# Lightning attention and a gated feed-forward: block 0 with two neighbouring tokens per partition, loads of 512 bytes, attention in 64x64 tiles, gate by tanh

## Chip, cores, metric

One core of one Trainium2 chip. The metric is the device time of the kernel in microseconds. Executions of one kernel mostly agree within 0.3%. Profiles are of one execution each.

## The reference

Attention with a decaying mask in blocks of 64, then a feed-forward layer with a sigmoid gate:

```python
# q, k, v: (4, 8, 768, 64) fp32; lam: (8,); w_gate, w_val: (512, 1536); w_out: (1536, 512)
for b in range(12):                                   # blocks of 64 tokens
    intra = einsum('bhic,bhjc->bhij', qb, kb) * Dmask # Dmask[i, j] = lam ** (i - j) for i >= j, else 0
    out   = intra @ vb + (qb * lam ** (i + 1)) @ kv_state
    kv_state = lam ** 64 * kv_state + (kb * lam ** (63 - i)).T @ vb
x    = out.transpose(0, 2, 1, 3).reshape(3072, 512)
gate = 1 / (1 + exp(-(x @ w_gate)))
y    = (gate * (x @ w_val)) @ w_out                   # (3072, 512) fp32
```

## The kernel before

It works in six steps of 128 tokens for all 4 batches and 8 heads. For each step, attention gives XT (512 token columns), twelve pairs of products gp = XT x w_gate and vp = XT x w_val follow, then the output product po. Attention of a later step runs between the products of the step ahead of it. Step 0 ("block 0") has nothing to hide behind: its loads and its attention are the start of the kernel, and the change is mostly about it.

```python
def load_hw(c, b, eng):                  # k of one batch, fp32, on a hardware queue
    H32[c, b] = hwp.tile([128, H, D], FP32, tag="h32", name="h32")
    eng.dma_start(out=H32[c, b], in_=src[b, :, 0:C, :].rearrange("h s d -> s h d"))

load_hw("k", 0, nc.sync)
nc.scalar.dma_start(out=lam_bc, in_=lam.partition_broadcast(128))
load_hw("k", 1, nc.scalar)
load(0, "q", 0, 2)                       # POOL queue, fp32 -> bf16, runs of 64 numbers
# [...] identity, index tables; k 2-3, q 2, q 3, v 0-1, v 2, v 3; weights

zeros(9)                                 # filler matmuls that keep TensorE busy
exponents(0)                             # VectorE: 4 of 128x128, mask exponents of the even heads
powers(0)                                # ScalarE: exp of them
cast_hw("k", 0)                          # VectorE: fp32 -> bf16
t_("k", 0, [0]); e_k(0, [0])             # TensorE transposes, ScalarE copy
exponents(1); cast_hw("k", 1); zeros(3); powers(1)
t_("q", 0, [0]); e_q(0, [0], nc.vector)
t_("q", 0, [1]); e_q(0, [1], nc.scalar)
t_("k", 0, [1]); e_k(0, [1])
# [...] scores and masks of batches 0, 1; transposes of 2, 3; scores and masks of 2, 3; outputs

def piece_gv(n, ft):                     # one of the twelve pairs of products
    # [...] gp and vp, four matmuls of 512 columns each
    nc.scalar.activation(sg, gp, AF.Sigmoid)
    nc.vector.tensor_mul(HT[n, ft], sg, vp)
```

## Time and profile before

| | before |
|---|---|
| time, median of 4 | 224.77 us |
| span of the profiled run | 222.8 us |
| first gp matmul of block 0 | 15.23 us |
| gapless start of TensorE (start of the fourth product, less 3 x 0.86 us for those before it) | 15.5 us |
| last matmul group (po) | 209.47 to 219.87 us |

The prediction shows the lines on what bounds this kernel: TensorE from 15 us on, the loads and the arithmetic of block 0 ahead of that. A line has the start, the duration, the engine, the line of code, the operation, and in brackets how long the engine sat idle before it and what ended that.

The list of transfers (`--dma`) has the time from issue to landing (last number, us) of the two loads of k, one batch each:

```profile
h<-in_k_dram SPq DMA_DIRECT2D x1, 256.0 KB, 4.1
h<-in_k_dram ACTq DMA_DIRECT2D x1, 256.0 KB, 4.5
```

SyncE's was issued at 0.74 and ScalarE's at 1.21 us.

### The profile page before, as it was taken

The page shows a single profiled execution, that of the slowest core. Times are in us where ns is not written, and L with a number is a line of the kernel's source. Part 1 is how long each engine was busy: PE and PEld are TensorE (multiplying, and loading weights), DVE is VectorE, ACT ScalarE, POOL GpSimd, SP SyncE. Part 2 cuts the span into 40 slices and gives each one's busy share as a digit, 9 for nine tenths or more (in the row PEclk, how much of TensorE's full clock was granted, in tenths as well). Part 3 has the DMA queues.
Part 4 walks back from the last instruction along what each step waited for, and adds up shares of the span by engine and source line. Part 5 has one row for each costly group of instructions (what it writes and reads, how often), then busy time and mean ns, then how long its engine had stood idle before and what let it go on. Part 6 is the DMA issues. An engine that isn't in the chain of part 4 may idle for free.

```text
span 222.8 us, 5208 instructions
## 1 busy us (share of the span) xinstructions
PE 215.8 (97%) x2187; PEld 105.7 (47%) x2187; DVE 104.4 (47%) x196; ACT 106.4 (48%) x232; POOL 64.0 (29%) x83
## 2 busy tenths in 40 slices
PE   6799999999999999999999999999999999999994
PEld 1454444557444544444544444544444544444443
DVE  4885652539777600785700686700676400333301
ACT  5877434594384523385433376342366342333221
POOL 7999855660094006700940030000000000000000
PEclk9999999999999999999999999999999999999999
DMA  6999999999989997999899995012100012100022
GB/s 108 152 169 182 195 203 178 175 156 156 176 55 158 235 153 214 179 162 176 56 157 231 223 63 36 3 50 94 47 3 0 3 50 94 47 0 0 4 94 96
DMA packets 106008, 25.25 MB, mean 113 GB/s; under 512 B 97152, under 2 KB 103552, under 8 KB 105984
## 3 DMA queue, kind: packets, MB, share of 16 engines
q0 software_dynamic: 82944, 13.90, 81.1%
q1 hardware_dynamic: 21712, 10.69, 20.4%
q10 hardware_dynamic: 1328, 0.33, 0.7%
q8 instruction: 17, 0.28, 0.5%
q14 instruction: 7, 0.06, 0.1%
HBM read 28.32 MB, written 6.29 MB: 155 GB/s over the span
## 4 chain that ended last, share of the span: by engine, by line
PE 91%; POOL 4%; DMA 3%; issue 1%; ACT 0%; POOLq 0%
PE po L523 28%; PE vp L488 28%; PE gp L488 28%; DMA WV<-in_moe_w_val_dram 3%; POOL vb L96 1%; PE sp L387 1%; PE cp L447 1%; PE op L411 1%; PE op L425 1%; POOL qb L96 1%; POOL WG L107 1%; POOL kb L96 1%; PE cp L363 1%; PE sp L310 0%; PE op L341 0%
## 5 line engine op out<-in xcount | busy, mean ns | idle before, releaser
L488 PE MATMUL gp<-XT,WG 128*128 128x512 bf16 (+1 forms) x296 | 74.2, 374 | 0.3 <-ACT XT L588 0.3
L488 PE MATMUL vp<-XT,WV 128*128 128x512 bf16 (+1 forms) x292 | 74.1, 376 | 0.1
L500 ACT ACTIVATE sg<-gp 128x512 bf16<-128x512 f32 x72 | 43.0, 597 | 62.9 <-PE gp L488 62.9
L505 DVE TENSOR_TENSOR ht<-sg,vp 128x512 bf16<-128x512 bf16 x48 | 33.0, 687 | 79.9 <-PE vp L488 76.9
L523 PE MATMUL po<-WO,ht 128*128 128x512 bf16 (+2 forms) x300 | 63.9, 371 | 0.0
L488 PEld LDWEIGHTS <-WV 128*128 128x128 bf16 x292 | 28.5, 98 | 33.7 <-DMA WV<-in_moe_w_val_dram 0.6
L523 PEld LDWEIGHTS <-ht 128*128 128x128 bf16 x300 | 28.3, 98 | 31.9
L488 PEld LDWEIGHTS <-WG 128*128 128x128 bf16 x296 | 28.2, 98 | 31.9 <-DMA WG<-in_moe_w_gate_dram 0.7
L527 ACT COPY ob<-po 128x512 f32<-128x512 f32 (+1 forms) x24 | 13.7, 572 | 38.8 <-PE po L523 38.8
L129 ACT ACTIVATE kd<-kb,kds 128x128 bf16<-128x128 bf16 (+1 forms) x88 | 28.9, 401 | 0.0
L503 DVE TENSOR_TENSOR ht<-sg,vp 128x512 bf16<-128x512 bf16 x24 | 16.5, 687 | 13.5 <-PE vp L488 13.3
L616 POOL COPY gates<-qt 128x1 bf16<-128x1 bf16 x4 | 0.8, 188 | 49.0 <-DMA qt<-qb 49.0
L96 POOL DMA_DIRECT2D vb<-in_v_dram x9 | 11.9, 1334 | 2.8 <-issue 1.7
L318 DVE TENSOR_TENSOR MT<-sp,mask 128x512 bf16<-128x512 f32 x16 | 9.9, 684 | 3.0 <-PE sp L310 3.0
L437 ACT CAST XT<-op 128x512 bf16<-128x512 f32 x16 | 8.2, 599 | 5.0 <-PE op L425 5.0
L397 DVE TENSOR_TENSOR MT<-sp,mask 128x512 bf16<-128x512 f32 x16 | 10.3, 683 | 0.0
L102 POOL DMA_DIRECT2D qb<-in_q_dram x10 | 8.8, 892 | 3.4 <-DMA WO<-in_moe_w_out_dram 3.2
L96 POOL DMA_DIRECT2D qb<-in_q_dram x8 | 8.9, 1115 | 1.8 <-POOLq L757 0.8
L102 POOL DMA_DIRECT2D kb<-in_k_dram x10 | 8.9, 913 | 1.1 <-DMA WG<-in_moe_w_gate_dram 0.6
L537 PE MATMUL zps<-st 128*128 128x512 bf16 x18 | 6.1, 471 | 1.5 <-DVE st L161 1.5
L96 POOL DMA_DIRECT2D kb<-in_k_dram x6 | 7.0, 1174 | 0.5 <-DMA WG<-in_moe_w_gate_dram 0.5
L110 POOL DMA_DIRECT2D WV<-in_moe_w_val_dram x9 | 7.1, 807 | 0.2 <-issue 0.2
(81 smaller groups left out, 114.3 us busy)
## 6 DMA issues: line engine op xcount, KB each, us to landing
out_dram<-ob SPq DMA_DIRECT2D x19, 256.0 KB, 2.3
vb<-in_v_dram POOLq DMA_DIRECT2D x4, 512.0 KB, 7.4
qb<-in_q_dram POOLq DMA_DIRECT2D x6, 256.0 KB, 7.7
kb<-in_k_dram POOLq DMA_DIRECT2D x6, 256.0 KB, 9.2
qb<-in_q_dram POOLq DMA_DIRECT2D x12, 128.0 KB, 7.5
WO<-in_moe_w_out_dram POOLq DMA_DIRECT2D x4, 384.0 KB, 12.3
kb<-in_k_dram POOLq DMA_DIRECT2D x10, 128.0 KB, 9.4
WG<-in_moe_w_gate_dram POOLq DMA_DIRECT2D x4, 256.0 KB, 7.0
```

Source lines behind the costliest of these rows:

```text
L96: nc.gpsimd.dma_start(out=T_[c, n][:, b0:nat], in_=src[b0:nat, :, sl, :].rearrange("b h s d -> s (b h) d"))
L102: nc.gpsimd.dma_start(out=T_[c, n][:, m:b1, u::2, :], in_=src[m:b1, 1 - u::2, sl, :].rearrange("b h s d -> s (b h) d"))
L129: nc.scalar.mul(KD[n][:, at, i, :], T_["k", n][:, at, i, :], kds[:, min(n // FIRST_XBAR, 1), h:h + 1])
L318: nc.vector.tensor_tensor(out=MT[n, b][:, u], in0=SP[n, b][u], in1=mask0[:, 1 - u if swapped(n, b) else u], op=ALU.mult)
L397: nc.vector.tensor_tensor(out=MT[n, bp][:, u], in0=SP[n, bp][u], in1=mask[:, u ^ bp].unsqueeze(1).to_broadcast([128, 2, HP, L]), op=ALU.mult)
L437: nc.scalar.copy(XT[n][:, c, :, bp * C:(bp + 1) * C], OP[n, c, bp].rearrange("p h j i -> p h (j i)"))
L488: nc.tensor.matmul(ps[:, part], lhsT=W[:, mt, fs], rhs=XT[n][:, part, mt], start=(part is not second and mt == 0), stop=(part is not first ...
L500: nc.scalar.activation(sg, gp.rearrange("p a b -> p (a b)"), AF.Sigmoid)
L503: mul = nc.vector.tensor_mul(HT[n, ft], sg, vp.rearrange("p a b -> p (a b)"))
L505: mul = nc.vector.tensor_mul(HT[n, ft].rearrange("p (b c i) -> p c b i", b=B, c=2), sg.rearrange("p (c b i) -> p c b i", c=2, b=B), vp.rea ...
L523: nc.tensor.matmul(po[:, :c1 - c0], lhsT=HT[n, ft][:, tt * 128:(tt + 1) * 128], rhs=WO[:, ft, c0:c1], start=(ft == 0), stop=(ft == NFT - 1))
L527: (eng.copy if eng is nc.scalar else eng.tensor_copy)(o, po[:, :c1 - c0])
```

## The change

Its intent: longer runs in the loads (a partition holds two neighbouring tokens of one head, 512 bytes in memory, 256 in the tile), so less time in the DMA engines; attention of block 0 in 64x64 tiles, which that layout asks for; tables that aren't needed at once moved behind the first products; and the gate by tanh, 0.5 (1 + tanh(x/2)), which shares a table with exp.

```diff
+    def pairs(src, b0, b1):
+        return src[b0:b1, :, 0:C, :].rearrange("b (r g) (p e) d -> g p b r (e d)", g=2, e=2)
+    def load0(c, b0, b1):               # two DMAs, one for each half of the partitions
+        for g in range(2):
+            nc.gpsimd.dma_start(out=T_[c, 0][rows_of(g), b0:b1]..., in_=src[g]...)
-    def load_hw(c, b, eng):             # k of one batch
+    def load_hw(g, eng):                # k of two batches, every second head
-    load_hw("k", 0, nc.sync)
+    load_hw(0, nc.sync)
     nc.scalar.dma_start(out=lam_bc, in_=lam.partition_broadcast(128))
-    load_hw("k", 1, nc.scalar)
-    load(0, "q", 0, 2)
+    load_hw(1, nc.scalar)
+    load0("q", 0, 2)
# [...] index tables for the new layout
+    nc.scalar.preload_act_table_set("exp_and_others")     # after the logs of lam
-    for hp in range(HP):                                  # moved behind the products
-        nc.scalar.activation(lamq[:, hp, :], ip1, AF.Exp, scale=lnp[:, 0, hp:hp + 1])
-    zeros(9)
+    zeros(8)
+    cast_hw(0)
     exponents(0)
     powers(0)
-    cast_hw("k", 0)
-    t_("k", 0, [0])
+    t_0("k", 0)
     e_k(0, [0])
+    zeros(2)
+    cast_hw(1)
     exponents(1)
-    cast_hw("k", 1)
-    zeros(3)
-    powers(1)
-    chunk_rows()
-    t_("q", 0, [0])
+    t_0("q", 0)
     e_q(0, [0], nc.vector)
+    powers(1)
# [...] the rest of block 0 the same way; s_0 and a_0: scores and outputs in 64x64 tiles
-        sg = htp.tile([128, TCH], BF16, tag="sg", name="sg", bufs=3)
+        sg = htp.tile([128, TCH], FP32, tag="sg", name="sg", bufs=3)
-                nc.scalar.activation(sg, gp..., AF.Sigmoid)
+                nc.scalar.activation(sg, gp..., AF.Tanh, scale=0.5)
-            mul = nc.vector.tensor_mul(HT[n, ft], sg, vp...)
+        mul = gate_value(HT[n, ft], sg, vp...)             # (sg + 1) * vp
-            (eng.copy if eng is nc.scalar else eng.tensor_copy)(o, po[:, :c1 - c0])
+            (eng.mul if eng is nc.scalar else eng.tensor_scalar_mul)(o, po[:, :c1 - c0], 0.5)
# [...] later tables, stores of block 0, token order of later blocks
```

## The prediction

> **What bounds the kernel now.** I read the page first: busy shares, then the chain that ended last.
>
> ```profile
> span 222.8 us, 5208 instructions
> PE 215.8 (97%) x2187; PEld 105.7 (47%) x2187; DVE 104.4 (47%) x196; ACT 106.4 (48%) x232; POOL 64.0 (29%) x83
> PEclk9999999999999999999999999999999999999999
> PE 91%; POOL 4%; DMA 3%; issue 1%; ACT 0%; POOLq 0%
> ```
>
> TensorE is busy for 97% of the span at full clock and carries 91% of the chain; VectorE and ScalarE are half idle. What isn't TensorE in the chain (POOL, DMA, issue) should therefore be one stretch. The chain in order of time shows it, at the start:
>
> ```profile
> 1.27 0.20 POOL qb L96
> ...
> 7.14 2.90 POOL vb L96 x3
> 10.04 0.75 POOL WG L107
> 10.79 0.74 POOL WV L110
> 11.53 0.67 POOL WG L107
> 12.21 5.81 DMA WV<-in_moe_w_val_dram
> 18.07 1.04 PE vp L488 x4
> 19.10 0.86 PE gp L488 x4
> ```
>
> From 18.07 us on every piece is PE, four matmuls in 0.86 us, up to the last copy at 219.89. Nothing there waits, so no cheaper vector, scalar or DMA work after 18 us can shorten the kernel; only what moves TensorE's start, or adds to TensorE's own work, can. In terms of gapless work, the start is 18.07 - 3 x 0.86 (the gp, vp, gp products before it) = 15.5 us. All that the change can win lies ahead of that. The timeline of TensorE and its weight loads says what held it:
>
> ```profile
> 14.52 0.25 PEld L585 LDWEIGHTS <-vb 128*64 128x64 bf16 x8 [0.44 <-DMA vb<-in_v_dram]
> 15.23 0.77 PEld L488 LDWEIGHTS <-WG 128*128 128x128 bf16 x8 [0.46 <-DMA WG<-in_moe_w_gate_dram]
> 18.06 0.55 PEld L488 LDWEIGHTS <-WV 128*128 128x128 bf16 x4 [0.55 <-DMA WV<-in_moe_w_val_dram]
> 15.23 1.05 PE L488 MATMUL gp<-XT,WG 128*128 128x256 bf16 x8 [0.30 <-ACT XT L588]
> ```
>
> The last v batch, the first gate weights and the second value weights each arrive just too late. But the first gp also waits for the last activation copy, which ends at that same 15.23. So transfers and arithmetic of block 0 end together: a faster transfer alone uncovers the arithmetic at once. This is the fact on which the prediction turns. The rates, by stretches (columns: PE, PEld, DVE, ACT, POOL busy, clock, DMA share, GB/s written):
>
> ```profile
> 5.00:13.00 8.00, 5.96 (x74) 3.42 (x73) 6.71 (x17) 7.14 (x17) 8.00 (x11) 1.00 2.37 156
> 14.00:24.00 10.00, 9.50 (x55) 4.56 (x54) 6.96 (x16) 7.20 (x16) 9.39 (x13) 1.00 1.71 184
> ```
>
> First q, k, v in runs of 64 numbers (256 bytes read, 128 written) at 156 GB/s, then weights in runs of 128 numbers at 184 GB/s. POOL, which makes the descriptors, is busy all the time, but a transfer lands 5 us or more after its issue, so the transfers, not the issue, are behind.
>
> **What the Trainium skill says.** "DMA: Bandwidth & Descriptors", section "Why small descriptors are slow (HBM only)": each packet costs about 3 cycles extra beside one per 32 bytes, 27% for 256 bytes; by that, doubling a run should win some 16%. The trace agrees roughly: 184/156 = 1.18. The same page's rules for kernel authors say that two transfers to disjoint partition halves gain nothing, since both use the same engines: so I give no gain for the split into halves itself, only for the longer runs. "ScalarE: Activation LUTs", section "Table sets: the hidden batching unit": exp and tanh share a set, exp and sigmoid don't, ln and exp share another; a load is put at 1283 ns, and the trace has 1.28 us for both of its loads (at 1.68 and 12.32). "TensorE: Matmul & The Clock Gate", section "Wait — 56ns, not 53.3ns?": 215.7 ns between warm matmuls of 512 columns; the chain's 0.86/4 = 0.216 agrees, so the steady part is already at its floor.
>
> **The change, part by part.**
>
> Transfers. k of two batches (0.52 MB, fp32) moves at about 263 GB/s from 4 to 5 us, some 2.0 us in all; with 512-byte runs I estimate 1.5. q, rest of k, and v write 1.31 MB: at 156 GB/s 8.4 us, at 184 GB/s 7.1. Together some 1.8 us earlier by the time the weights start: last v near 12.5 instead of 14.5, first gate weights near 13.3, second value weights near 16. Issue: eight DMAs of 512 descriptors, at the 0.80 us of the weight issues of 512 descriptors, make 6.4 us; before, seven issues on POOL (1.28, 1.18, 0.95 twice, 1.16, 0.90 twice) made 7.4. The weight issues start near 9.7 instead of 10.0. POOL is nearly the bound then, but not for a need of 17 us.
>
> Head of the arithmetic. Removed: the swap matrix, the matmul that swaps halves and its 0.68 us copy, four small logs, four exponentials (1.28 us on ScalarE at 4.9 to 6.1), three small tables (0.8 us), six small vector operations. Most go to later steps of block 0's feed-forward, where both engines have room: the heaviest two get four 0.32 us activations beside the 0.60 of the gate, 1.9 us in a step of 1.73, twice; two steps of slack swallow that. Added: a table load after the logs, 4.55 to 5.85, in the very place of the exponentials; the load at 12.32 goes.
>
> Then the order. Each k cast now needs both half transfers, and the first cast comes ahead of the exponents. Say both halves are there at 4.8 (before, landing took 4.1 and 4.5 us from issues at 0.74 and 1.21, so 5.2 to 5.3 on average). VectorE: cast 0.41, two exponents of 256 columns, cast 0.64, two more. One exponent took 0.29 in a row of four at 128 columns; 1.0 ns a column (copies of 512 and 256 columns: 681 and 424 ns) makes 0.42. Sum 2.73: 7.5. ScalarE: powers 0.62, q copy 0.59, k copy 0.59, overlapping about 0.1: the k copy ends at 9.2. Before, it ended at 9.17. From there before: 0.83 until the next k copy (score matmuls, transposes), 2.3 us for four copies. Score matmuls in 64x64 tiles are 32 instead of 8 per batch: four run together, 53 ns per round of 128 columns, eight rounds, 0.43 us instead of 0.21. So +0.1 on the first step: copies from 10.1 to 12.4. Last scores done 12.9. Masking (eight multiplications, 0.62 us apart) ends near 14.2, as the last two follow the last scores. Output matmuls: sixteen per batch, two together at most, 0.43 us instead of 0.21; four batches in order, 13.1 to 14.8. Last copies 0.42 us behind: 15.3; the first half of gp (0.43 us) fits in between. Gapless start: about 14.9.
>
> Steady part. Gate by tanh: one activation of 512, still 0.60 us. The product takes three operands and an fp32 gate, still one element a cycle because vp is in PSUM: about 0.69, at most 0.75 (the three-operand row stands near 0.34 for 128 columns, two-operand copies 0.05 below that). One per 1.73 us. Copies times 0.5 cost a copy. Permuted copy of the activations: 0.60 still, not on the chain. State products at the end of block 0's first pass: 64 small matmuls instead of 32; 61 of that kind took 0.71 against 0.62 now: +0.1 us on TensorE. Output stores: same bytes.
>
> Sum: 14.9 - 15.5 + 0.1 = -0.5 us: 224.82 - 0.5 = 224.3.
>
> **The rivals.** (1) The transfers were all that mattered, and the full 1.8 us come home: 223.0. For: three waits on DMA stand on TensorE's loads. Against: the copy ending at 15.23, and ScalarE busy without a gap from 10.7 to 12.9. (2) The arithmetic of block 0 becomes the bound and is longer: two k halves must land, the table load lies between logs and powers, tiles of 64x64 take twice the rounds. If k lands at 5.4 instead of 4.8, everything slides by 0.6: 224.9, no gain. For: the chain of casts, exponents, powers and copies has no slack in my sum. (3) Issue on POOL becomes the bound: 64-partition issues at 1.0 us each would start the weights at 11.3 and land the second value weights near 16.5; still in time for 17.5; no loss, unless issues cost 1.3 or more. (4) Something in the steady part stalls TensorE: a table switch at each gate, or the product holding a PSUM bank beyond the 1.73 us step. A switch per step would add 1.28 us to ScalarE's 0.60 and hurt by tens of us; exp and tanh being one set speaks against it.
>
> **Range and chances.** The front can't win more than about 2 us: even with all inputs in place VectorE needs 5 us of masking after the first scores near 8. Rivals 1 and 2 set the ends: 223.2 to 225.1. 2% is 4.5 us, more than the front can give; only rival 4 could lose as much. Faster 0.01, same 0.97, slower 0.02.
>
> **What would show it.** Right: the first gp near 14.7 to 15.2, waiting for an activation copy and not for weights; no wait of weight loads on WV; qkv stretches near 184 GB/s; one table load near 4.6; 0.86 per four matmuls unchanged. Step by step: the second k copy on ScalarE ending near 9.2, score groups of 32 in 0.6 us, output groups 0.43 apart. Wrong: gp first at 13.5 or before (rival 1), after 15.5 (rival 2), weights waited for (rival 3), any TensorE gap after the start (rival 4).

## More of the kernel before

```profile
3.95 0.21 ACT L192 ACTIVATE lns<-lam_bc 128x8 f32<-128x8 f32 x1 [0.98 <-DMA lam_bc<-in_lam_dram]
4.28 1.17 DVE L211 SCALAR_TENSOR_TENSOR mask<-dij,lns,neg 128x128 f32<-128x128 f32 x4 [1.04 <-ACT lns L192]
5.37 0.41 DVE L293 CAST kb<-h 128x512 bf16<-128x512 f32 x1
8.59 0.59 ACT L288 COPY KS<-tk 128x512 bf16<-128x512 bf16 x1
```

VectorE does mask work as soon as lam is there, and the first cast of k, at 5.37, has no bracket: k's first batch landed while VectorE was busy with the mask. The wait for k costs nothing here.

## The result

| | before | after |
|---|---|---|
| time, median of 4 | 224.77 us | 225.28 us |
| span of the profiled run | 222.8 us | 223.5 us |
| first cast of k | 5.37 us | 6.20 us |
| second k copy on ScalarE | 8.59 to 9.18 us | 9.80 to 10.39 us |
| first gp matmul | 15.23 us | 16.14 us |
| gapless start of TensorE | 15.5 us | 16.2 us |

The ratio is 1.0023 (95% interval 1.0006 to 1.0040). The change made the kernel a quarter of a per cent slower: the class (within 2%) was as predicted, the direction and the range were not.

First the page of the kernel after (span, busy shares, the chain by engine), then its chain in order of time.

```profile
span 223.5 us, 5462 instructions
PE 217.2 (97%) x2312; PEld 107.2 (48%) x2312; DVE 103.4 (46%) x192; ACT 107.8 (48%) x236; POOL 63.6 (28%) x85
PE 95%; DMA 2%; ACT 1%; DVE 0%; ACTq 0%; issue 0%; DVEq 0%
```

```profile
1.16 4.94 DMA h<-in_k_dram
6.20 0.44 DVE kb L358
6.68 0.64 PE tk L285 x8
7.31 0.97 PE zps L601 x2
8.28 1.01 PE tq L285 x15
9.32 0.59 ACT QS L340
...
14.31 1.91 PE op L311 x64
16.21 1.05 PE gp L553 x8
17.26 0.86 PE vp L553 x4
```

POOL and the weights have left the chain; from 17.26 on it is TensorE alone as before, at the same 0.86 us per four matmuls. At its head now stands one transfer, the second half of k, issued at 1.16 and landed 4.94 us later. The timeline shows what hung on it:

```profile
6.20 0.43 DVE L358 CAST kb<-h 128x512 bf16<-128x512 f32 x1 [1.96 <-DMA h<-in_k_dram]
7.25 1.03 PE L601 MATMUL zps<-st 128*128 128x512 bf16 x2
7.45 0.63 ACT L221 ACTIVATE mask<-mask 128x512 f32<-128x512 f32 x1 [1.75 <-DVE mask L216]
8.21 1.06 PE L285 MATMUL tq<-ident,qb 128*64 128x128 bf16 x16
9.80 0.59 ACT L353 COPY KS<-tk 128x512 bf16<-128x512 bf16 x1
14.24 1.97 PE L311 MATMUL op<-MT,vb 64*64 64x128 bf16 x64
16.14 0.84 PEld L553 LDWEIGHTS <-WG 128*128 128x128 bf16 x8
```

VectorE sits idle for 1.96 us and ScalarE for 1.75, although lam, from which the mask is made, is there at 3.75. The cast of k was put ahead of the mask exponents in VectorE's order, so the mask work waits for k too. The gate weights, which the kernel before waited for (0.46 us at 15.23), are there in time: the line at 16.14 has no bracket. So the weights are earlier, and it buys nothing; k is not, as its second half landed at 6.10 and the second load of k before at 5.7. The rate of the transfers, from the table by stretches (last column GB/s written), answers to the 156 GB/s of before:

```profile
5.00:11.50 6.50, 4.61 (x91) 3.05 (x90) 4.12 (x10) 3.76 (x7) 6.50 (x10) 1.00 1.78 176
```

The three-operand product of the gate took 687 ns against 686 to 687 of the two-operand one, in the groups of lines:

```profile
L543 DVE SCALAR_TENSOR_TENSOR ht<-sg,vp 128x512 bf16<-128x512 f32 x72 | 49.4, 687 | 93.0 <-PE vp L553 89.1
```

### The profile page after: what moved, and what is told of

It reads as the page before. It is cut to its first block, busy times and chain, and to the rows that moved or that the text cites. A ratio compares the mean times of both kernels' runs of the same rounds, so it can differ in the third digit from the quotient of the medians.

```text
span 223.5 us, 5462 instructions
## 1 busy us (share of the span) xinstructions
PE 217.2 (97%) x2312; PEld 107.2 (48%) x2312; DVE 103.4 (46%) x192; ACT 107.8 (48%) x236; POOL 63.6 (28%) x85
## 4 chain that ended last, share of the span: by engine, by line
PE 95%; DMA 2%; ACT 1%; DVE 0%; ACTq 0%; issue 0%; DVEq 0%
PE gp L553 28%; PE po L587 28%; PE vp L553 28%; DMA h<-in_k_dram 2%; PE sp L449 1%; PE cp L509 1%; PE zps L601 1%; PE op L473 1%; PE op L487 1%; PE op L311 1%; PE tq L285 1%; PE tk L285 1%; PE sp L295 0%; PE sp L375 0%; PE op L406 0%; PE tq L277 0%
## 5 line engine op out<-in xcount | busy, mean ns | idle before, releaser
L543 DVE SCALAR_TENSOR_TENSOR ht<-sg,vp 128x512 bf16<-128x512 f32 x72 | 49.4, 687 | 93.0 <-PE vp L553 89.1
L565 ACT ACTIVATE sg<-gp 128x512 f32<-128x512 f32 x72 | 43.0, 597 | 59.3 <-PE gp L553 59.3
L591 ACT ACTIVATE ob<-po 128x512 f32<-128x512 f32 (+1 forms) x24 | 14.0, 583 | 38.6 <-PE po L587 38.6
L143 ACT ACTIVATE kd<-kb,kds 128x128 bf16<-128x128 bf16 x80 | 25.2, 392 | 0.0
L459 DVE TENSOR_TENSOR MT<-sp,mask 128x512 bf16<-128x512 f32 x16 | 10.3, 682 | 0.0
L96 POOL DMA_DIRECT2D vb<-in_v_dram x6 | 9.0, 1504 | 3.3 <-issue 1.6
L102 POOL DMA_DIRECT2D qb<-in_q_dram x10 | 8.8, 890 | 3.1 <-DMA WO<-in_moe_w_out_dram 2.8
L102 POOL DMA_DIRECT2D kb<-in_k_dram x10 | 8.9, 911 | 1.0 <-DMA WG<-in_moe_w_gate_dram 0.6
L118 POOL DMA_DIRECT2D WG<-in_moe_w_gate_dram x8 | 6.8, 847 | 0.0
L534 DVE SCALAR_TENSOR_TENSOR st<-st,pow_l,cp 128x128 bf16<-128x128 bf16 x24 | 6.7, 341 | 0.0
L96 POOL DMA_DIRECT2D kb<-in_k_dram x5 | 5.9, 1177 | 0.5 <-issue 0.5
L96 POOL DMA_DIRECT2D qb<-in_q_dram x5 | 5.8, 1150 | 0.5 <-DMA WO<-in_moe_w_out_dram 0.5
```

The lines of the kernel that those rows point to most:

```text
L96: nc.gpsimd.dma_start(out=T_[c, n][:, b0:nat], in_=src[b0:nat, :, sl, :].rearrange("b h s d -> s (b h) d"))
L102: nc.gpsimd.dma_start(out=T_[c, n][:, m:b1, u::2, :], in_=src[m:b1, 1 - u::2, sl, :].rearrange("b h s d -> s (b h) d"))
L143: nc.scalar.mul(KD[n][:, at, i, :], T_["k", n][:, at, i, :], kds[:, min(n // FIRST_XBAR, 1), h:h + 1])
L459: nc.vector.tensor_tensor(out=MT[n, bp][:, u], in0=SP[n, bp][u], in1=mask[:, u ^ bp].unsqueeze(1).to_broadcast([128, 2, HP, L]), op=ALU.mult)
L543: return nc.vector.scalar_tensor_tensor(out=o, in0=g, scalar=1.0, in1=x, op0=ALU.add, op1=ALU.mult)
L565: nc.scalar.activation(sg, gp.rearrange("p a b -> p (a b)"), AF.Tanh, scale=0.5)
```

## The experiments

Theories, as formed from these two traces: **A**, k's late landing and the serial order behind it (cast, exponents, powers, copies) set the start; **B**, TensorE ran at half speed between 6.7 and 9.3 us (two fillers in 1.03 us, sixteen transposes in 1.06) and that set it; **C**, the 64x64 tiles of the output matmuls set it. All runs were timed in 5 rounds. Every result was correct.

| run | time (median) | before, same rounds | ratio, 95% interval | first k cast | first gp |
|---|---|---|---|---|---|
| (after the change) | 225.28 | 224.77 | 1.0023 (1.0006 to 1.0040) | 6.20 | 16.14 |
| e1_exp_first | 225.63 | 224.74 | 1.0043 (1.0027 to 1.0059) | 6.38 | 16.46 |
| e2_no_zeros2 | 227.40 | 224.74 | 1.0123 (1.0105 to 1.0141) | 6.30 | 17.77 |
| e3_both | 225.94 | 224.74 | 1.0046 (1.0020 to 1.0072) | 6.24 | 16.75 |
| e4_warm | 225.76 | 224.74 | 1.0035 (1.0023 to 1.0047) | 6.27 | 16.07 |
| e5_k_sooner | 226.14 | 224.64 | 1.0072 (1.0047 to 1.0096) | 5.57 | 18.19 |
| e8_before_tanh | 224.76 | 224.64 | 1.0004 (0.9992 to 1.0016) | - | 15.46 |
| e9_masks_first | 224.37 | 224.64 | 0.9988 (0.9976 to 1.0000) | 6.32 | 15.27 |
| e10_masks_a | 224.17 | 224.64 | 0.9976 (0.9964 to 0.9988) | 6.34 | 15.34 |
| e11_best | 224.45 | 224.56 | 1.0000 (0.9985 to 1.0014) | 6.62 | 15.29 |
| e12_q_later | 224.60 | 224.56 | 1.0004 (0.9992 to 1.0016) | 6.28 | 15.34 |
| e14_k_by_batch | 224.67 | 224.56 | 1.0003 (0.9991 to 1.0015) | 5.94 | 14.95 |
| e15_all | 224.75 | 224.56 | 1.0007 (0.9994 to 1.0020) | 5.93 | 15.04 |
| e16_k_now | 226.12 | 224.69 | 1.0062 (1.0034 to 1.0090) | 5.84 | 15.89 |
| e17_masks_k_now | 226.94 | 224.69 | 1.0097 (1.0084 to 1.0110) | 7.91 | 17.75 |
| e18_all | 226.67 | 224.69 | 1.0084 (1.0071 to 1.0097) | 7.60 | 17.13 |
| e19_masks_a_11 | 224.15 | 224.69 | 0.9980 (0.9968 to 0.9992) | 6.20 | 14.86 |
| e20_k_batch_plain | 224.95 | 224.71 | 1.0010 (0.9997 to 1.0022) | 4.72 | 15.26 |
| e21_k_later | 225.88 | 224.71 | 1.0050 (1.0036 to 1.0063) | 6.93 | 16.72 |

The times of the last two columns are those of the one profiled run; where runs of one kernel scatter (e1, e2, e3, e5, e16 by 1.3 to 2 us, e11 by 1.1), it need not be the median run.

### First round: the order of the mask work, and the speed of TensorE

**e1_exp_first**

```diff
     zeros(8)
-    cast_hw(0)
     exponents(0)
+    exponents(1)
+    cast_hw(0)
     powers(0)
     t_0("k", 0)
     e_k(0, [0])
     zeros(2)
     cast_hw(1)
-    exponents(1)
     t_0("q", 0)
     e_q(0, [0], nc.vector)
     powers(1)
```

> After the change with one move: all four mask exponents on VectorE ahead of the first cast of k, in the 1.96 us that VectorE idles until k lands at 6.2 us. Theory A (the late k and the serial order cast, exponents, powers, copies set the start): the powers are done near 7.0 instead of 9.3, the copies of q and k on ScalarE start about 1 us earlier, first gate matmul near 15.2 instead of 16.14, about 224.3 us. Theory B (TensorE is cold after waiting 1.55 us for k: two filler matmuls take 1.03 us and sixteen transposes 1.06 us): the second q transposes still end near 9.3, the q copy behind them too, and the gain is under 0.2 us: about 225.2. Theory C (the 64x64 tiles at the end, 64 matmuls in 1.97 us, set the start alone): also no gain.

Measured 225.63, no gain. The exponents did go into the hole (4.35 to 6.02 on VectorE), but powers(1) stood behind the first k copy in ScalarE's order and began at 8.08 only. TensorE was fast when k came (two fillers in 0.61 us at 7.49) but then fell back until 11.4 us (the sixteen transposes at 10.70 took 1.05 us), and the clock row of the page reads 7 tenths in its second slice (5.6 to 11.2 us). The run moved half of what it should have moved; it doesn't decide.

**e2_no_zeros2** takes out `zeros(2)`.

> After the change without the two filler matmuls between the first k transposes and the first q transposes. Theory A: the powers on ScalarE end at 9.28 us as before and hold the q copy: no gain, 225.2 to 225.3. Theory B: the q transposes end 0.9 us earlier and so does everything: about 224.4. If both are true side by side (the two paths end within 0.05 us of each other, 9.28 and 9.29), no gain.

**e3_both** is e1 and e2 together.

> Both moves at once: exponents ahead of the casts, and no filler matmuls before the q transposes. If two paths of equal length run side by side, neither move alone gains and this one does: the q copy on ScalarE near 8.4 instead of 9.32, first gate matmul near 15.2, about 224.3 us. Theory A alone expects the same as of the first run, theory B alone the same as of the second; theory C expects 225.2.

**e4_warm** has `zeros(13)` instead of `zeros(8)`.

> After the change with 13 instead of 8 filler matmuls at the start, so that TensorE has no gap of 1.55 us while k lands. If its clock was down because of that gap, the two fillers later take about 0.43 us instead of 1.03, the sixteen transposes 0.64 instead of 1.06, and the TensorE path is about 0.9 us shorter. Theory B: about 224.4 us. Theory A or two equal paths: no gain, 225.2, as the powers still end at 9.28.

e2 lost 2 us, which no theory had expected. Three lines of TensorE's timeline in e2, and then two in e4:

```profile
7.36 1.07 PE L285 MATMUL tq<-ident,qb 128*64 128x128 bf16 x16
13.93 0.58 PE L295 MATMUL sp<-QS,KS 64*64 64x128 bf16 x16
17.77 1.11 PE L553 MATMUL gp<-XT,WG 128*128 128x256 bf16 x8
```

```profile
7.64 0.64 PE L285 MATMUL tq<-ident,qb 128*64 128x128 bf16 x16
16.07 1.12 PE L553 MATMUL gp<-XT,WG 128*128 128x256 bf16 x8
```

Sixteen transposes take 1.07 us in e2 and 0.64 in e4: the speed of TensorE is real. Without the two fillers it stayed low up to 14.4 us, and every transpose and score ahead of that was slower. So the fillers are no dead weight, and B is right that speed matters. But e4, with TensorE fast from 6.75 on, has its first gp at 16.07 against 16.14: TensorE's slow phase alone did not set the start of the changed kernel. In e4 the second k copy ends at 10.31, against 10.39, because powers(1) on ScalarE still begin at 8.72: the two paths are equally long. The five runs of e4 fall in two groups, two at 225.2 (the profiled one is among them) and three at 225.8, and no profile shows why. e3 is then no clean test of both, as it has the slow TensorE of e2 (sixteen transposes in 1.06 us twice); its six runs lie between 224.89 and 226.84.

### Second round: the mask work out of the way

**e9_masks_first** keeps TensorE busy and puts all mask work ahead of k, on both engines:

```diff
-    zeros(8)
-    cast_hw(0)
+    zeros(13)
     exponents(0)
     powers(0)
+    exponents(1)
+    powers(1)
+    cast_hw(0)
     t_0("k", 0)
     e_k(0, [0])
     zeros(2)
     cast_hw(1)
-    exponents(1)
     t_0("q", 0)
     e_q(0, [0], nc.vector)
-    powers(1)
```

> 13 fillers, and the mask work of both halves (four exponents on VectorE, two powers on ScalarE) ahead of all work on k, in the time in which k is still on its way. In the first of the runs the second powers stood behind the first k copy on ScalarE and TensorE was slow until 11 us; both are mended here. Theory A in its mended form (k's landing, the serial mask work behind it, and a TensorE whose speed must be kept up): second k copy ends near 9.1 instead of 10.3, first gate matmul near 15.0, 224.3 us. If the 64x64 tiles at the end or the weights set the start, it stays at 16.0 and 225.2 to 225.8.

224.37 us. ScalarE, VectorE and TensorE in e9:

```profile
5.69 1.15 ACT L221 ACTIVATE mask<-mask 128x512 f32<-128x512 f32 x2
6.32 0.92 DVE L358 CAST kb<-h 128x512 bf16<-128x512 f32 x2 [0.30 <-DMA h<-in_k_dram]
8.85 0.59 ACT L353 COPY KS<-tk 128x512 bf16<-128x512 bf16 x1
15.27 1.11 PE L553 MATMUL gp<-XT,WG 128*128 128x256 bf16 x8
```

k lands as late as ever (6.32), the powers are done at 6.84, the second k copy ends at 9.44 instead of 10.39, and the first gp comes 0.87 us earlier than after the change and 0.80 earlier than in e4. Only the order in which instructions stand differs from e4, and the profiled runs differ by as much (224.42 and 225.24): the serial mask work behind k is shown to be worth 0.8 us.

**e10_masks_a** also moves the output matmuls of batches 0 and 1 ahead of the last scores, and drops `zeros(3)` there:

```diff
     s_0(2)
-    zeros(3)
+    a_0(0, ...); a_0(1, ...)
     s_0(3)
     zeros(1)
-    for b in range(B):
+    for b in range(2, B):
         a_0(b, ...)
```

> As the run before, and the output matmuls of batches 0 and 1 put ahead of the last scores, in place of three fillers. Of the 1.97 us that the 64 output matmuls take in one run at the end, half is out of the way; what remains behind the last mask product is one batch, 0.5 us. Theory C (the tiles of 64x64 cost at the end): first gate matmul 0.3 us earlier than in the run before, near 14.7, 224.0 us. If VectorE's last mask product sets the end, under 0.1 us. If weights become the bound, TensorE waits for WG or WV.

224.17 against 224.37 in the same rounds: 0.2 us, a little short of the 0.3 expected and not much more than the scatter (the runs of e10 reach up to 224.45, those of e9 down to 224.26). In the profiled run the thirteen fillers ran slow to the end (5.72 us) and held the first transposes up to 7.19, which hides the gain there: counted from the first transposes, the first gp comes after 8.15 us in e10 and after 8.47 in e9. C is a small part. With 11 fillers (**e19_masks_a_11**, fourth round) it is 224.15, with the first gp at 14.86 (8.17 after the first transposes), no different within the scatter, and as expected:

> Reference: mask work first, output matmuls earlier, lam on the ScalarE queue as in the change, 11 fillers instead of 13: 224.0 to 224.2 us, as with 13 (224.17).

**e8_before_tanh** is the gate alone in the kernel before: tanh, fp32 gate, three-operand product, copies times 0.5, token order of later blocks by the copy of XT.

```diff
-                nc.scalar.activation(sg, gp..., AF.Sigmoid)
+                nc.scalar.activation(sg, gp..., AF.Tanh, scale=0.5)
-            mul = nc.vector.tensor_mul(HT[n, ft], sg, vp...)
+            mul = nc.vector.scalar_tensor_tensor(out=HT[n, ft], in0=sg, scalar=1.0, in1=vp..., op0=ALU.add, op1=ALU.mult)
# [...] copies times 0.5, XT in token order; one table load as before, of the exp set
```

> The kernel before with the gate part of the change alone: tanh of half the argument with an fp32 result, a three-operand product, copies times 0.5, and the token order of later blocks made by the copy of the activations. All of it beside TensorE work that waits for nothing: 224.7 to 224.9 us, within 0.1 of the kernel before. If the gate part costs or gains at all, the difference shows here: a slower product (0.75 instead of 0.69 us) would not show.

224.76 against 224.64, ratio 1.0004: the gate costs nothing and gains nothing by itself. What it makes possible, one table for exp and tanh, matters only if the start is bound there.

**e5_k_sooner** is e4 with lam's load behind k's second half on the ScalarE queue instead of ahead of it.

> Compared with the run of 13 fillers (225.76 us; first gate matmul at 16.07, TensorE fast from 6.7 us on): the second half of k is issued ahead of lam on the ScalarE queue, so at 0.74 instead of 1.16 us. Theory A (the start hangs on the landing of the second half of k, then cast, exponents, powers, copies in series): the first cast moves from 6.27 to about 5.9, the first gate matmul to about 15.7, 225.3 us or a little under. Rival (ScalarE is tied to lam: logs, then a table load, then powers): lam is 0.4 us later, the table load ends near 6.1 instead of 5.7 but the powers start at 7.1 at the soonest, so no change from this side; if the start hangs on anything else than k, 225.7.

k came sooner (cast at 5.57), but the time went up. The line that says why:

```profile
6.41 0.42 ACT L200 ACTIVATE lns<-lam_bc 64x4 f32<-64x4 f32 x2 [2.95 <-DMA lam_bc<-in_lam_dram]
```

lam, 4 KB, landed 2.7 us later than ahead of k (3.71 in e4), and logs, table load and powers with it. The expected 0.4 us was wrong by far: behind 256 KB in the same queue a small load waits for them. So the run says nothing on k. Its profiled run is the slow one of a pair (227.53 of 225.7 to 227.7), and TensorE fell back to half speed in it at 12 us, which the clock row of its page shows (third slice). It shows the same of e1, e17 and e18, and of no run the slow start, where it reads 9:

```profile
PEclk9969999999999999999999999999999999999999
```

### Third round: why k is late, and better versions

**e12_q_later** is e9 with `load0("q", 0, 2)` behind the identity and the index table on POOL.

> Why k lands at 6.1 to 6.3 us and not at the 4.8 of the prediction. Base: the run with the mask work first and 13 fillers (k's cast at 6.32, first gate matmul 15.27, 224.37 us). Here the loads of q for batches 0 and 1 are issued after the identity and the index table, some 0.7 us later. Contention theory (q's packets, issued in two halves from 1.26 us on, take turns with k's on the 16 engines): k's second half lands 0.3 to 0.7 us sooner, cast at 5.6 to 6.0, but q lands 0.7 later, near 7.7, so the q transposes wait and the time is 224.2 to 224.7. Rival (the half-partition form of k's own transfers, whose issues take 0.77 and 0.70 us instead of 0.45, and the later start of the second): the cast stays at 6.3 within 0.1.

The cast stays at 6.28. q's packets are not what makes k late, at least not those of the first 0.3 us by which the issue moved (1.26 to 1.57; less than the 0.7 that I had written). The rival came true in its number, but no run isolates the form of k's transfers, so why k's second half takes 4.9 to 5.1 us is not shown. The time, 224.60, is level with the kernel before.

**e14_k_by_batch** is e9 with 10 fillers and k's load split by batch:

```diff
-    load_hw(0, nc.sync)
     nc.scalar.dma_start(out=lam_bc, in_=lam.partition_broadcast(128))
-    load_hw(1, nc.scalar)
+    for b in range(2):
+        load_hw(b, 0, nc.sync)          # one batch, one half of the heads
+        load_hw(b, 1, nc.scalar)
```

> Same base, but k is loaded by batch as in the kernel before (four transfers of one batch and one half of the heads each, two on each queue), so that the first cast needs the first batch alone; 10 fillers instead of 13. Theory A (the wait for both halves of k is the step that failed): first cast near 5.2 to 5.6 instead of 6.3, first k copy on ScalarE near 6.5 instead of 7.26; behind it q (landing about 7.0 to 7.6) becomes the next wait, so the first gate matmul gains 0.2 to 0.5 us, 223.9 to 224.2 us. If TensorE becomes slow with the fewer fillers, 225 or more.

The first cast comes at 5.94, now right behind the exponents, the first k copy at 6.92 instead of 7.26, and the first gp at 14.95, 0.32 us before that of e9. But the time is 224.67. In the profile of e14 the last store is issued 0.30 us sooner than in e9 (219.74 against 220.04), while the span is 0.2 us longer (222.8 against 222.6). The other two runs with four k transfers (e15, e20) have the same half microsecond after the last store; no run with two has it. No instruction or transfer that the trace shows lies there. Its cause stays open.

**e11_best** is e10 with 11 fillers and lam on the SyncE queue ahead of k's first half; **e15_all** is e10 with 10 fillers, k by batch, and lam on the SyncE queue.

> Mask work first, output matmuls of two batches ahead of the last scores, 11 fillers, and lam on the SyncE queue ahead of the first half of k, so that the second half is issued at 0.74 us without putting lam behind k (which cost 2.3 us of lam's landing in the run with k sooner). k's last landing near 5.7 instead of 6.1 to 6.3, the first gate matmul 0.3 to 0.4 us earlier than with 13 fillers: near 14.9, 223.8 to 224.0 us. If the TensorE path behind is bound by q (landing near 7.2), nothing is gained: 224.2.

> Everything at once: mask work first, output matmuls earlier, k by batch, lam on the SyncE queue, 10 fillers. 223.7 to 224.0 us if k's landing still counts behind the mask work; 224.2 if q's landing or TensorE's speed takes over.

e11 missed: the half of k that stands behind lam lands last, whichever queue it is; the cast came at 6.62, and the median 224.45 is no gain on e10. e15 has its first gp at 15.04 and loses it again at the end, as e14 does.

### Fourth and fifth round: k's landing by itself

**e16_k_now**: the change's order, 11 fillers, lam's load issued from POOL, so that both k halves are issued at 0.74. **e17_masks_k_now**: the same with the mask work first. **e18_all**: with the earlier output matmuls too.

```diff
     load_hw(0, nc.sync)
-    nc.scalar.dma_start(out=lam_bc, in_=lam.partition_broadcast(128))
     load_hw(1, nc.scalar)
+    nc.gpsimd.dma_start(out=lam_bc, in_=lam.partition_broadcast(128))
```

> The change's own order, with lam loaded from POOL (ahead of q, which the run with q later showed to be harmless), so that both halves of k are issued at 0.74 us on SyncE and ScalarE without standing before lam; 11 fillers. If k's landing is the failed step: first cast near 5.5 instead of 6.2 to 6.3, first gate matmul 0.6 to 0.7 us earlier than in the run of 13 fillers (16.07), near 15.4, 224.5 us. If the serial mask work or lam holds the chain instead: cast at 5.5, gate matmul at 15.9 or later, 225.1 or more.

> Mask work first and k's halves issued at 0.74 us, lam from POOL, 11 fillers. lam lands near 4 us, powers end near 7.0, the first cast comes near 6.0 behind the four exponents on VectorE, so about 0.3 us is to be had against the run with the mask work first (15.27): first gate matmul near 14.9 to 15.0, 224.0 us. If lam from POOL lands late (5 us or more), the powers end after 8 and nothing is gained.

> As the run before with the output matmuls of batches 0 and 1 ahead of the last scores: another 0.2 to 0.3 us, first gate matmul near 14.7, 223.7 to 223.9 us.

All three missed, and their profiles show one reason: lam from POOL was there at 5.6 to 5.9 (3.7 from the ScalarE queue). With the mask work first this does the most harm: in e17 the casts wait behind exponents that wait for lam, 7.91 us, and TensorE is slow again until 12 us. The last sentence of the expectation of e17 had allowed for it. e16's profiled run (225.10) has powers(0) right behind the table load at 7.54, so lam, not k, held it; three of its six runs are at 225.1 to 225.4 and three at 226.8 to 227.0, which no profile explains.

The last two runs move k and leave lam alone. **e20_k_batch_plain** is e4 with k by batch (as in e14). **e21_k_later** is e4 with both halves of k on one queue:

```diff
-    load_hw(1, nc.scalar)
+    load_hw(1, nc.sync)
```

> The change's own order, 13 fillers, k by batch, lam where the change has it (landing near 3.8). Theory A (k's landing is the step that failed): first cast near 5.3 instead of 6.27, powers about 0.6 to 0.9 us earlier, second k copy near 9.6 instead of 10.3, first gate matmul near 15.4 instead of 16.07. The time would be 224.7, or 225.1 if the longer end of the other two runs by batch (0.4 to 0.5 us after the last matmul, cause unknown) comes with it. Rival (something else sets the start): gate matmul at 16.0.

> The change's own order, 13 fillers, both halves of k on the SyncE queue, so that the second is issued at about 1.5 instead of 1.16 us; lam unchanged. Theory A: the first cast moves from 6.27 to about 6.6 and the first gate matmul by as much, to about 16.4; 225.6 to 226.1 us. Rival: gate matmul stays at 16.07 within 0.1.

Cast and first gp, e20 and then e21:

```profile
4.72 0.43 DVE L359 CAST kb<-h 128x512 bf16<-128x512 f32 x1 [0.50 <-DMA h<-in_k_dram]
15.26 1.12 PE L554 MATMUL gp<-XT,WG 128*128 128x256 bf16 x8
```

```profile
6.93 0.43 DVE L358 CAST kb<-h 128x512 bf16<-128x512 f32 x1 [2.71 <-DMA h<-in_k_dram]
16.72 1.12 PE L553 MATMUL gp<-XT,WG 128*128 128x256 bf16 x8
```

Against e4 (cast 6.27, gp 16.07): k 0.66 us later, gp 0.65 later; k's first batch 1.55 us earlier, gp 0.81 earlier, as the second batch, cast at 6.67, then holds the second half of the mask work. This is theory A, shown in both directions with nothing else touched. The time of e21, 225.88 with all its runs within 0.13, agrees with e4's profiled run (225.24), from which those gp times come; the median of e4, which lies in its slower group, is only 0.12 lower. e20 has 224.95, with the half microsecond at the end.

## Why the prediction was wrong, point by point

- **What bounds the kernel** held: after the first gp no time was won or lost. The gapless start moved by 0.75 us and the span of the profiled runs by 0.7 (the medians by 0.5).
- **"So transfers and arithmetic of block 0 end together: a faster transfer alone uncovers the arithmetic at once"** held. Rates rose from 156 to 176 GB/s (184 said), no weight load waited any more, and nothing came of it. (ScalarE, "busy without a gap from 10.7 to 12.9" before, was so up to 13.60, with its table load.)
- **The step that failed: "Say both halves are there at 4.8."** In the profile of the kernel before the two loads of k landed at 4.8 and 5.7; 4.8 is the landing of the first, or the "5.2 to 5.3 on average" of the text less the half microsecond that it expects of longer runs. But the changed cast waits for the last of the two, not for the first or the mean. And the half microsecond (2.0 to 1.5 us, 25%) is more than the text's own 16 to 18%; between 4 and 5 us the trace after shows 283 GB/s for all transfers together against 263, 8% more. Measured: the second half landed 4.94 us after its issue at 1.16, so at 6.10, with the cast at 6.20, 1.4 us later than said: 0.9 for waiting for the last, 0.4 because that last landed later than before (why is not shown), 0.1 from landing to cast. The first gp came at 16.14 instead of about 14.8, 1.3 us later. e21 shows that shift one to one, e20 takes most of it back.
- **"The chain of casts, exponents, powers and copies has no slack in my sum"** (rival 2) was the way it went, but its size, "if k lands at 5.4", was too small; the range ended at 225.1 for that reason. The chain itself was priced well: from first cast to the end of the second k copy 4.4 us said, 4.2 measured; from there to the first gp about 5.6 said, 5.75 measured.
- What the prediction saw and did not use: the cast was put ahead of the exponents. It noted the new order and did not ask what VectorE does until k lands. The answer (1.96 us idle, with lam there) is worth 0.8 us by e9 against e4.
- **TensorE's speed** was not in the prediction at all. In the changed kernel it was slow until 9.3 us, as long as the path on the other engines, so it explains no part of the miss alone (e4); with fewer fillers it cost 2 us (e2).
- **64x64 tiles**: the scores are 16 matmuls per batch, as the code has it, not the 32 of the text; at full speed they took 0.42 us where the eight of before took 0.40, so they got no dearer (0.43 instead of 0.21 was said), and the likeness to the 0.43 is chance. The outputs took 1.97 us for four batches against 1.7 said. These two misses have opposite signs, so the close sum from cast to gp is in part luck. Half of the outputs done earlier is worth about 0.2 us (e10).
- **Gate by tanh, tables moved, state products**: as said. 0.69 us the product, no stall, 0.64 against 0.62 us for the state products (0.1 more was said), nothing in the time (e8).
- **POOL's issue** (rival 3) was no bound: the weight issues began at 8.89, as half-partition issues took 0.70 to 0.81 (9.7 said; but the text's own issues, 6.4 us against the 7.3 to which its seven durations add up, it wrote 7.4, give 9.1).

The change by itself: weights that are issued over a microsecond earlier (8.89 instead of 10.00) with nobody waiting for them; a start that waits for the last of two transfers instead of the first; and a mask that waits with it. Of the versions that put the mask work first, with two transfers of k and lam on a hardware queue, e9, e10 and e19 run at 224.15 to 224.37 us, 0.1 to 0.25% under the kernel before (ratios 0.9976 to 0.9988 with intervals that reach 1.0000 at most), and e12, with q later, is level (1.0004), as is e11, with lam moved (1.0000). So with the order mended the new layout is no slower than the old.

## What to carry to other kernels

When a change merges or splits transfers, list for each first use which transfers it needs now, and take the landing of the last one from the trace, not the mean. Work that needs another input than the late one belongs ahead of it in every engine's order (here the mask work stood behind the cast of k while VectorE sat idle for 1.96 us); look at where the idle time in brackets lies before asking how fast anything is. Fillers on TensorE are part of the timing: take them out only with an eye on the durations of the matmuls behind them.

## What the Trainium skill lacked or had wrong

- "TensorE: Matmul & The Clock Gate", section "What's actually happening", puts the speed-up after about one busy window of 3.4 us, varying by 500 ns. Here unbroken fillers sped up within 4.3 us (thirteen in 4.29 us in e9) in one run, and not within 5.7 us (thirteen in 5.72 us in e10) in another of the same first 7 us; and after eight fillers (3.59 us) and a wait of 1.55 us, sixteen transposes still took 1.06 us instead of 0.64 (after).
- The same page, section "Part 4: PE-mode transpose", says that transposes don't count as busy for the clock in the same way. The runs neither confirm nor refute it: e2 and e3 fit it (mostly transposes and scores from 6.8 us on, TensorE busy for 84% and 92% of the time up to the three fillers, and slow for over 6 us), but no run isolated it.
- "ScalarE: Activation LUTs", section "What ACT_TABLE_LOAD costs", adds a drain of some 1380 ns to each load of 1283 ns. In e9 the load runs from 4.39 to 5.67, the activation before it ends at 4.38 and the next starts at 5.69: no drain is seen.
- "DMA: Bandwidth & Descriptors", section "Anatomy of one DMA — SWDGE (gpsimd) path", fits 2.0 us plus bytes over 436 GB/s for a DMA from that path. A 4 KB load from POOL took 4.3 to 4.6 us while k was under way (e16, e17); on the hardware queue 3.0 (after, e9), and behind 256 KB on that queue 4.9 (e5).
- No page says how the issue time on the hardware queues depends on the shape of a transfer: one of 128 partitions took 0.45 us to issue (before), one of 64 partitions with the same bytes in runs twice as long 0.70 and 0.77 (after).
- No page has, and I can't explain, the half microsecond after the last store in the three runs with four instead of two transfers of k (3.1, 3.0 and 3.0 us from the issue of the last store to the end of the span in e14, e15, e20; 2.6 in e9).
